# Halves of a head as even and odd channels: the regrouping of v's weights as 32-bit words on VectorE

## The chip, the core and the metric

One core of one Trainium2 chip runs the kernel. The metric is the device time of one execution in microseconds (us), as the median of three runs.

## The reference, cut to what matters

Two independent parts share one output of 2048 rows: columns 0 to 575 are part A, a sliding attention of 32 heads with 18 channels each, over 8 positions at a distance of 2; columns 576 to 1151 are part B, a long convolution.

```python
S, D, H, Dh, W, dil = 2048, 576, 32, 18, 8, 2
q, k, v = heads(x @ wqkv)                      # part A
logits = einsum("bhsd,bhswd->bhsw", q, k[idx]) * Dh ** -0.5      # idx = s - 2w, masked below 0
o = einsum("bhsw,bhswd->bhsd", softmax(logits), v[idx])
a = o.reshape(B, S, D) @ wo
k_shift = sum of 4 shifted copies of k, each times shift_k       # part B
kv = k_shift * v
b = q * (causal_convolution(kv, ssm_k) + kv * ssm_D)             # by FFT in the reference
```

## The kernel before, in words

TensorE (PE) multiplies, VectorE (DVE) makes elementwise products, ScalarE (ACT) evicts PSUM and does exponentials, GpSimd (POOL) and SyncE (SP) issue DMAs.

Part A. x is transposed to xT. `project` (L377 to L411) makes q, k and v transposed, 128 channels by 1024 positions at a time, in PSUM tiles ps_proj that ACT evicts (L411). For the logits, DVE multiplies q by shifted k (L827, 20 products, 10 for each half of the positions), PE sums the products over the 18 channels of a head into ps_log (L842), and ACT evicts ps_log (L847). `softmax` (L870 to L887) works on DVE, with the exponential (L876), the logarithm (L883) and its negative exponential (L884) on ACT. DMAs of SP spread the weights (L931). DVE multiplies them by v (L953), PE sums over the 8 positions into ps_acc (L970, L984), and ps_wo (L1025, L1017) multiplies by wo, which six DMAs of POOL load (L1001, L1004).

For that product a head's 18 channels of v are held as two halves, 9 channels each: partition 2h + s holds half s of head h, one channel of the half in each group of 64. So the columns of v's weights must stand in another order than in memory. They land raw in the tile Ks, and `regroup` (L895) copies them into xw: five instructions of ACT, one for each block of 128 rows, each 128x576 bf16 read with a stride of 9 elements (18 bytes). Half 0 is channels 0 to 8 of a head, half 1 channels 9 to 17, and the rows of wo are loaded in the same order.

Part B. DVE applies the four taps (L574, L578, L594); PE folds (ps_fold, evicted at L606); the filter is folded as well (ps_rev, evicted at L673); matrices of sines turn both into spectra: `filter_spectrum` (ps_fk, L624 and L625, evicted at L690) and `x_spectrum` (ps_fx, L771, evicted at L773). Each spectrum has two parts and their sum as a third. The sum is made by DMAs, or by DVE at once in a whole add of 128x2304 (`add_third`, L1058), or, where that has not been done when the first product of a block needs it, in a piece of 128x768 (L1240). DVE multiplies spectra (L1095), PE sums products into ps_z (L1122) and transforms back (ps_inv L1154, ps_back L1195), and DVE multiplies by q.

The order of each engine's work is that in which the code issues it. Units of PE work with their evictions wait in a queue, `units`. The code calls `until()` at some 47 places, and the table PLACES says how many units are issued at each. FKS and FXS say how x spectra, filter spectra and projections of v stand behind each other in the queue, AT where the folds stand, PRE and ZMIX where the whole adds and the first products of spectra stand between the last products with v. REGROUP says where the five regroups stand in the queue. PSUM tiles come in two kinds, A and B, of two tiles each; ps_proj and ps_rev use A, ps_log and ps_acc B, and the spectra either.

Of the kernel before, what the change touches and what calls it, by code (L numbers as in the profile page):

```python
# [18 lines left out]
ZMIX = (  # L19
    1, 1, 2, 0, 0, 6,  # L20
)

PRE = (
    22, 16,
)

THIRDS = ((0, 1),), ((0, 2), (1, 2)), ((0, 3), (1, 3))

REGROUP = (
    2, 0, 0, 17, 17,  # L30
)

PLACES = (
    4, 19, 7, 8, 3, 0, 6, 4, 8, 3, 12, 3, 3, 1, 4, 4, 3, 4, 2, 4, 0, 5, 5, 6, 2, 4, 3, 2, 1, 0, 3, 1, 2, 2, 3, 1,
    0, 3, 2, 8, 10, 3, 0, 1, 13, 1, 1, 0,
)

FKS = (
    6, 0, 0, 0, 0, 0, 0, 0, 0, 0, 0, 0, 0, 0, 0, 0, 0, 0, 0, 0, 1, 0, 0, 2, 0, 0, 0, 0, 0, 0,
)  # L40
FXS = (
    7, 0, 0, 5, 1, 0, 0, 6, 1,
)

EARLY = (
# [1 line left out]
)  # L47

AT = (
    0, 5, 31,  # L50
)
# [8 lines left out]
def kernel(  # L60
# [13 lines left out]
    nc = tc.nc  # L74
    Bsz, S, D = A_x.shape
# [50 lines left out]
    xw = main.tile([128, 12 * HB], BF16, name="xw")  # L126
# [11 lines left out]
    def xT(kb, t0, n):  # L138
        return view(xw, HB * (3 + 3 * (t0 // 1024)) + 1024 * kb + t0 % 1024, [[1, n]])
# [41 lines left out]
    Ks = main.tile([128, 12 * HB], BF16, name="Ks")  # L181
# [3 lines left out]
    def k_at(m, part):  # L185
        return 3 * HB * (3 - m) + HB * part
# [128 lines left out]
    q, k = qk[:, 0:4 * S + 1024], qk[:, 4 * S + 1024:]  # L315
# [56 lines left out]
    def project(comp, jj):  # L372
        def body(ps, ct, jj, jp, first):
            for kb in range(4):
                se = dict(start=(kb == 0 and not first), stop=(kb == 3 and first))
                if ct < 4:
                    nc.tensor.matmul(ps[:, jp, :], wq(kb, comp, 128 * ct, 128), xT(kb, 1024 * jj + 512 * jp, 512), **se)  # L377
                    continue
                for e in range(2):
                    w = wq(kb, comp, 512, 64)  # L380
                    nc.tensor.matmul(ps[64 * e:64 * e + 64, jp, :], w, xT(kb, 1024 * (jj if ct < 4 else e) + 512 * jp, 512),
                                     tile_position=(0, 64 * e), **se)

        def tails(ps, ct, jj, first):
            se = dict(start=first, stop=not first)
            if ct < 4:
                for r in range(2):
                    nc.tensor.matmul(ps[:, r, :], wq(4, comp, 128 * ct, 128)[64 * r:64 * r + 64],  # L388
                                     x5(jj)[64 * r:64 * r + 64], tile_position=(64 * r, 0), **se)
                return  # L390
            for e in range(2):
                w = wq(4, comp, 512, 64)
                for r in range(2):
                    nc.tensor.matmul(ps[64 * e:64 * e + 64, r, :], w[64 * r:64 * r + 64],
                                     x5(jj if ct < 4 else e)[64 * r:64 * r + 64], tile_position=(64 * r, 64 * e), **se)

        def unit(ct, jj, jp, first, box):
            t, o, pad = dest(comp, ct)
            if jp == 0:
                box["ps"] = bank2("ps_proj", "A")  # L400
                if first:
                    tails(box["ps"], ct, jj, True)
            ps = box["ps"]
            body(ps, ct, jj, jp, first)
            if jp == 0:
                clk["P"] += 1.15 if first else 0.9
                return
            if not first:
                tails(ps, ct, jj, False)
            pe(0.9 if first else 1.15, "A", 1.02)  # L410
            nc.scalar.activation(view(t, o + pad + 1024 * jj, [[512, 2], [1, 512]]), ps[:], ACT.Copy)  # L411
            if ct == 4 and comp > 0:
                (nc.gpsimd if comp == 1 else nc.sync).dma_start(view(t, o, [[1, PAD]])[64:128, :], view(t, o + 1024, [[1, PAD]])[0:64, :])

        for ct in range(4) if jj < 2 else [4]:
            first = ct % 2 == 1 if ct < 4 else comp == 1
            box = {}
            for jp in range(2):
                units.append((0.9 + 0.25 * (jp != first), partial(unit, ct, jj % 2, jp, first, box),
                              f"v{jj}{ct}" if comp == 2 else f"proj{comp}"))  # L420
# [208 lines left out]
    def row(m, c):  # L629
        return kTok(m)[0:1, c, :]  # L630
# [20 lines left out]
    def negate(*ms):  # L651
        for m in ms:
            signed.add(m)
            dve(288, lambda: nc.vector.tensor_scalar(minus_of(m), spare(m) if m < 2 else row(m, 0), -0.5 * ROOT, None,
                                                     ALU.mult))
# [26 lines left out]
    def filter_spectrum(m):  # L682
        def unit(gi, cs):
            tag = filler_tag("fk", "AAB") if logits_run[0] else "A"
            ps = bank2("ps_fk", tag)
# [4 lines left out]
            nc.scalar.activation(view(Ks, k_at(m, cs ^ (m & 1)) + 96 * gi, [[768, 3], [384, 2], [1, 96]]), acc3(ps),  # L690
                                 ACT.Copy, scale=(PSG, MSG)[cs][m] * 2.0 ** 1.5 / 1024.0)
# [23 lines left out]
    raw = view(Ks, k_at(0, 0), [[D, 5], [1, D]])  # L715

    for i in range(NBL):
# [30 lines left out]
        for n, u in enumerate(mirrors):  # L748
            n = AT[n] if n < 2 else AT[i]
# [140 lines left out]
    def steps(gen, n):  # L890
        for _ in range(n):
            next(gen, None)

    def regroup(kb):
        nc.scalar.activation(view(xw, w_at(kb, 2), [[64, 9], [1, 64]]), view(raw, D * kb, [[1, 9], [9, 64]]), ACT.Copy)  # L895
        clk["A"] += 0.65

    until()
    la, lb = logits(0), logits(1)
    logits_run[0] = True  # L900
    for kb in range(5):
        units.insert(REGROUP[kb], (0.0, partial(regroup, kb), "regroup"))
    steps(la, 3)
    negate(1, 0)
    steps(la, 10)
    steps(lb, 1)
    sa = softmax(0, view(av, 2048, [[1, 1024]]), view(av, 3072, [[1, 512]]))
    steps(sa, 1)
    steps(lb, 3)
    steps(sa, 1)  # L910
    steps(lb, 1)
    steps(sa, 1)
# [84 lines left out]
    wo = view(qk, WO, [[2 * D, 2], [D, 2], [1, D]])  # L997
    woh = view(qk, WO + 4 * D, [[1, D]])
    for e in range(2):
        for b in range(2):  # L1000
            nc.gpsimd.dma_start(wo[64 * e:64 * e + 64, :, b, :],  # L1001
                                bass.AP(tensor=A_wo.tensor, offset=A_wo.offset + ((0, 3), (2, 1))[e][b] * D,
                                        ap=[[9 * D, 64], [4 * D, 2], [1, D]]))
# [338 lines left out]
```

## Time and profile before

| what | us |
|---|---|
| median of 3 runs (range) | 215.75 (215.73 to 215.81) |
| the profiled execution | 215.78 |
| its span, first to last instruction | 214.0 |
| PE busy | 200.8 |
| DVE busy | 191.0 |
| ACT busy | 156.4 |
| POOL busy | 72.0 |

The busy times are sums over one profiled execution. A matmul's end is modelled, so a busy PE need not be at its peak. Times within the execution count from the span's start. In rows of single instructions the square bracket at the end is the idle time of the engine just before the instruction, with what ended it.

### The profile page before, as it was taken

Reading aid. Unit: us, or ns where it says so; the run is one execution under the profiler, and the core shown is the slowest. Engines: PE = TensorE matmul, PEld = TensorE weight load, DVE = VectorE, ACT = ScalarE, POOL = GpSimd, SP = SyncE. Lnnn points to the kernel's source line nnn. Section 1 sums busy time; section 2 is a strip of 40 time slices with the busy share of each in tenths; the row PEclk is TensorE's granted clock in tenths of the full one; section 3 lists DMA queues with packets and bytes.
Section 4 is the critical chain, followed back from the end, with each engine's and each line's share of the span. In section 5 each row is a group of like instructions: output and inputs, shape, how many; then the busy total and the mean of one; then the engine's idle time right before and its main releaser. Section 6 shows DMA issues by size and latency. Waiting matters only on the chain.

```text
span 214.0 us, 5106 instructions
## 1 busy us (share of the span) xinstructions
PE 200.8 (94%) x2122; PEld 111.6 (52%) x2122; DVE 191.0 (89%) x142; ACT 156.4 (73%) x223; POOL 72.0 (34%) x107
## 2 busy tenths in 40 slices
PE   7999999999877898999999999999989999999891
PEld 3543443445644555563336456655655667676560
DVE  7989999999979987766989999899999869979981
ACT  3799975686899999975459868855765887575640
POOL 8999992102292509220074000002009204033000
PEclk9999999999999999999999999999999999999997
DMA  6999999899566416999979989395659996965233
GB/s 209 292 321 228 279 321 296 204 162 191 124 83 87 63 23 93 192 161 187 231 172 237 197 181 219 69 205 180 140 196 298 246 307 143 214 188 161 87 110 110
DMA packets 35332, 39.66 MB, mean 185 GB/s; under 512 B 17555, under 2 KB 28943, under 8 KB 35310
## 3 DMA queue, kind: packets, MB, share of 16 engines
q1 hardware_dynamic: 26812, 24.88, 47.0%
q0 software_dynamic: 6032, 11.95, 29.6%
q10 hardware_dynamic: 2466, 2.51, 3.7%
q8 instruction: 16, 0.26, 0.5%
q14 instruction: 6, 0.05, 0.1%
HBM read 13.11 MB, written 4.72 MB: 83 GB/s over the span
## 4 chain that ended last, share of the span: by engine, by line
PE 55%; ACT 10%; DVE 1%; issue 1%; DVEq 0%
PE ps_z L1122 9%; PE ps_wo L1025 8%; PE ps_inv L1154 7%; PE ps_acc L970 7%; PE ps_proj L377 7%; PE ps_fx L771 5%; ACT Ks L690 4%; PE ps_log L842 3%; PE ps_fk L624 2%; PE ps_wo L1017 1%; ACT qk L974 1%; PE ps_proj L388 1%; ACT xw L895 1%; PE ps_acc L984 1%; DVE TB L1163 1%; ACT av L847 1%
## 5 line engine op out<-in xcount | busy, mean ns | idle before, releaser
L377 PE MATMUL ps_proj<-xw 128*128 128x512 bf16 x160 | 37.6, 380 | 0.5 <-ACT TI L456 0.5
L827 DVE TENSOR_TENSOR av<-qk 128x4096 bf16<-128x4096 bf16 (+1 forms) x16 | 31.9, 2020 | 4.9 <-PE ps_log L842 4.7
L377 PEld LDWEIGHTS <-xw 128*128 128x128 bf16 x160 | 14.5, 97 | 19.7 <-issue 4.6
L690 ACT ACTIVATE Ks<-ps_fk 128x576 bf16<-128x576 f32 x32 | 19.4, 737 | 1.3 <-PE ps_fk L625 1.0
L411 ACT ACTIVATE qk<-ps_proj 128x1024 bf16<-128x1024 f32 x14 | 14.4, 1026 | 7.9 <-PE ps_proj L388 3.6
L1095 DVE TENSOR_TENSOR qk<-xw,Ks 128x2304 bf16<-128x2304 bf16 x14 | 18.5, 1354 | 1.3 <-PE ps_z L1122 1.2
L574 DVE TENSOR_TENSOR tB<-kj,skb 128x4608 bf16<-128x4608 bf16 (+1 forms) x8 | 19.3, 2418 | 0.1
L1135 ACT ACTIVATE av<-ps_z 128x768 bf16<-128x768 f32 x20 | 15.3, 809 | 5.4 <-PE ps_z L1122 5.4
L773 ACT ACTIVATE xw<-ps_fx 128x576 bf16<-128x576 f32 x32 | 19.1, 667 | 0.2 <-PE ps_fx L771 0.2
L771 PE MATMUL ps_fx<-xw,TB 128*128 128x288 bf16 x128 | 17.9, 287 | 1.3 <-ACT xw L606 1.2
L624 PE MATMUL ps_fk<-Ks,TB 128*128 128x384 bf16 x62 | 16.7, 326 | 1.9 <-ACT Ks L673 0.9
L1051 POOL DMA_DIRECT2D Ks<-Ks x3 | 3.6, 1217 | 43.4 <-PE ps_wo L1025 32.3
L1025 PE MATMUL ps_wo<-qk 128*128 128x288 bf16 x128 | 17.9, 287 | 0.0
L411 ACT ACTIVATE v<-ps_proj 128x1024 bf16<-128x1024 f32 x9 | 9.5, 1055 | 8.8 <-PE ps_proj L377 5.4
L771 PEld LDWEIGHTS <-TB 128*128 128x128 bf16 x128 | 11.8, 98 | 7.6 <-issue 4.5
L970 PE MATMUL ps_acc<-av,ident 64*64 64x512 bf16 x160 | 15.3, 378 | 0.0
L625 PE MATMUL ps_fk<-Ks,TB 128*128 128x192 bf16 x62 | 15.2, 245 | 0.0
L1025 PEld LDWEIGHTS <-qk 128*128 128x128 bf16 x128 | 11.5, 98 | 5.7 <-issue 3.0
L1157 ACT ACTIVATE v<-ps_inv 128x576 bf16<-128x576 f32 (+1 forms) x14 | 9.5, 675 | 6.6 <-PE ps_inv L1154 6.6
L1154 PE MATMUL ps_inv<-av,TI 128*128 128x288 bf16 (+1 forms) x96 | 13.6, 293 | 0.6 <-ACT av L1135 0.6
L953 DVE TENSOR_TENSOR av<-Ks,v 128x4096 bf16<-128x4096 bf16 x6 | 13.6, 2287 | 0.6 <-PE ps_acc L970 0.6
L974 ACT ACTIVATE qk<-ps_acc 128x1024 bf16<-128x1024 f32 x8 | 8.2, 1023 | 7.5 <-PE ps_acc L970 7.5
(199 smaller groups left out, 473.9 us busy)
## 6 DMA issues: line engine op xcount, KB each, us to landing
Ks<-Ks POOLq DMA_DIRECT2D x9, 576.0 KB, 7.0
TB<-av SPq DMA_DIRECT2D x12, 256.0 KB, 5.4
kj<-in_B_k_dram SPq DMA_DIRECT2D x6, 504.0 KB, 6.2
vt<-in_B_v_dram SPq DMA_DIRECT2D x8, 288.0 KB, 5.1
Ks<-av SPq DMA_DIRECT2D x8, 256.0 KB, 5.6
Ks<-Ks SPq DMA_DIRECT2D x3, 576.0 KB, 5.1
Ks<-in_A_x_dram SPq DMA_DIRECT2D x2, 576.0 KB, 5.2
xw<-in_A_wqkv_dram SPq DMA_DIRECT2D x2, 576.0 KB, 5.9
```

Source lines behind the costliest of these rows:

```text
L377: nc.tensor.matmul(ps[:, jp, :], wq(kb, comp, 128 * ct, 128), xT(kb, 1024 * jj + 512 * jp, 512), **se)
L411: nc.scalar.activation(view(t, o + pad + 1024 * jj, [[512, 2], [1, 512]]), ps[:], ACT.Copy)
L574: dve(2304 * n, lambda: nc.vector.tensor_tensor(to, view(kj, row * D, [[D, n], [D, 4], [1, D]]), view(skb, row * D, [[D, n], [0, 4], [1, D ...
L624: nc.tensor.matmul(o[:, 0:2], w, rhs[:, 0:2], start=start, stop=stop)
L690: nc.scalar.activation(view(Ks, k_at(m, cs ^ (m & 1)) + 96 * gi, [[768, 3], [384, 2], [1, 96]]), acc3(ps), ACT.Copy, scale=(PSG, MSG)[cs][ ...
L771: nc.tensor.matmul(ps[:, pm, 0:HD], TX[:, 2 * pm + c, 128 * gi:128 * gi + 128], kv[:, 2 * c + pm, HD * h:HD * h + HD], start=(c == 0), sto ...
L773: nc.scalar.activation(view(xw, HB * XG[i] + 96 * gi + 1152 * h, [[HB, 2], [384, 3], [1, 96]]), view(ps, 0, [[512, 2], [96, 3], [1, 96]]), ...
L827: return P, at, step, dve(1024 * nj, lambda: nc.vector.tensor_tensor(view(P, at, [[step, 4], [256, nj], [1, 256]]), view(t, o + 256 * hh, ...
L970: nc.tensor.matmul(acc[64 * o:64 * o + 64, h, :], ident[64 * h:64 * h + 64, 64 * h:64 * h + 64], view(P, 256 * u, [[2048, 2], [1, 256]])[6 ...
L1025: nc.tensor.matmul(ps[:, r, 0:HD], oT(hh, 2 * c + r, t)[:, o:o + 128], wo[:, t // 2, t % 2, HD * h:HD * h + HD], start=(t == 0 and h == 0) ...
L1122: nc.tensor.matmul(view(acc[r], 512 * h, [[192, 2], [96, 2], [1, 96]])[o:o + 64], w[64 * h:64 * h + 64, 64 * h:64 * h + 64], pr[64 * h:64 ...
L1154: nc.tensor.matmul(ps[:, c, 0:n], TI[:, sl, pm, 128 * c:128 * c + 128], Y(j, pm)[:, sl, c0:c0 + n], start=(pm == 0 and sl == 0), stop=(sl ...
```

## The change

The halves of a head become its even and its odd channels. Two neighbouring channels of 16 bits then are one word of 32 bits, and both halves keep the order of the words: the regroup copies words (0..8, head) in place of single channels. It is done by DVE with a bitwise or with zero, four blocks of 128 rows in one instruction (128x1152 words) and the fifth in another (128x288), each read with a stride of 9 words (36 bytes). ACT's five instructions go. The two are called just ahead of the first unit that projects v, or ahead of a unit of the last filter's spectrum, or at a place in the list of steps, whichever comes first. wo is loaded in the matching order of rows, in ten DMAs in place of six. Eight tables have other numbers.

```diff
 REGROUP = (
-    2, 0, 0, 17, 17,
+    15, 14,
 )
...
 FXS = (
-    7, 0, 0, 5, 1, 0, 0, 6, 1,
+    0, 0, 15, 0, 8, 0, 0, 4, 0,
 )
...
             if jp == 0:
                 box["ps"] = bank2("ps_proj", "A")
+                while comp == 2 and regroups:
+                    regroups.pop(0)()
...
-    def regroup(kb):
-        nc.scalar.activation(view(xw, w_at(kb, 2), [[64, 9], [1, 64]]), view(raw, D * kb, [[1, 9], [9, 64]]), ACT.Copy)
-        clk["A"] += 0.65
-
+    def regroup(k0, n):
+        src, to = (view(t, at, [[1, n * D]]).bitcast(I32) for t, at in ((Ks, k_at(0, 0) + D * k0), (xw, w_at(k0, 2))))
+        dve(576 * n, lambda: nc.vector.tensor_single_scalar(
+            to.rearrange("p (k a h) -> p k a h", k=n, a=9), src.rearrange("p (k h a) -> p k a h", k=n, a=9), 0,
+            ALU.bitwise_or))
+
+    regroups.extend([partial(regroup, 0, 4), partial(regroup, 4, 1)])
...
-            nc.gpsimd.dma_start(wo[64 * e:64 * e + 64, :, b, :],
-                                bass.AP(tensor=A_wo.tensor, offset=A_wo.offset + ((0, 3), (2, 1))[e][b] * D,
-                                        ap=[[9 * D, 64], [4 * D, 2], [1, D]]))
+            for u in range(2):
+                nc.gpsimd.dma_start(wo[64 * e:64 * e + 64, u, b, :],
+                                    bass.AP(tensor=A_wo.tensor, offset=A_wo.offset + (((0, 6), (4, 2))[e][b] + 8 * u) * D,
+                                            ap=[[18 * D, 32], [D, 2], [1, D]]))
```

What the tables move is seen in the order of the engines' instructions (line, operation, out<-in, size, and how often in a row). ACT before, from the first regroups, behind the last fold and three evictions of ps_fx, to the row ahead of the second eviction of logits; one L690 and that L847 follow:

```order
L773 ACTIVATE xw<-ps_fx 128x2x3x96 x3
L895 ACTIVATE xw<-Ks 128x576 x2
L773 ACTIVATE xw<-ps_fx 128x2x3x96 x2
L895 ACTIVATE xw<-Ks 128x576
L773 ACTIVATE xw<-ps_fx 128x2x3x96
L690 ACTIVATE Ks<-ps_fk 128x6x96 x2
L673 ACTIVATE Ks<-ps_rev 128x576 x2
L690 ACTIVATE Ks<-ps_fk 128x6x96
L847 ACTIVATE av<-ps_log 128x1024
L690 ACTIVATE Ks<-ps_fk 128x6x96 x7
L895 ACTIVATE xw<-Ks 128x576 x2
L673 ACTIVATE Ks<-ps_rev 128x576 x2
```

ACT now, from the same fold to the second eviction of logits (L414 is L411 of before, L778 is L773, L695 is L690, L676 is L673, L852 is L847):

```order
L414 ACTIVATE v<-ps_proj 128x1024 x2
L778 ACTIVATE xw<-ps_fx 128x2x3x96
L695 ACTIVATE Ks<-ps_fk 128x6x96
L778 ACTIVATE xw<-ps_fx 128x2x3x96
L695 ACTIVATE Ks<-ps_fk 128x6x96
L676 ACTIVATE Ks<-ps_rev 128x576 x2
L852 ACTIVATE av<-ps_log 128x1024
L695 ACTIVATE Ks<-ps_fk 128x6x96 x8
L676 ACTIVATE Ks<-ps_rev 128x576 x2
L695 ACTIVATE Ks<-ps_fk 128x6x96
L852 ACTIVATE av<-ps_log 128x1024
```

The regroups are gone, four of six evictions of ps_fx have moved behind, and two projections of v have come forward, to the place behind the last fold.

DVE now, where the taps of part B end (the L597) and the logits begin; before, the two L901 are not there and the other rows are the same:

```order
L597 TENSOR_TENSOR xw<-xw,vt 128x2304
L657 TENSOR_SCALAR Ks<-Ks 1x576 x2
L901 TENSOR_SCALAR xw<-Ks 128x1152
L901 TENSOR_SCALAR xw<-Ks 128x288
L832 TENSOR_TENSOR av<-qk 128x4096 x2
L832 TENSOR_TENSOR v<-qk 128x4x1024
L657 TENSOR_SCALAR Ks<-Ks 1x576
```

Both regroups stand ahead of the first logits product.

DVE before, where the first products of spectra (L1095) come between the last products with v (L953):

```order
L1058 TENSOR_TENSOR xw<-xw 128x2304
L953 TENSOR_TENSOR av<-Ks,v 128x4096 x2
L953 TENSOR_TENSOR qk<-TB,v 128x4096
L1240 TENSOR_TENSOR Ks<-Ks 128x768
L1095 TENSOR_TENSOR Ks<-xw,Ks 128x2304
L953 TENSOR_TENSOR av<-TB,v 128x4096
L1058 TENSOR_TENSOR Ks<-Ks 128x2304
L1095 TENSOR_TENSOR Ks<-xw,Ks 128x2304
```

DVE now at the same place (L1062 is L1058 of before, L956 is L953, L1244 is L1240, L1099 is L1095):

```order
L956 TENSOR_TENSOR av<-Ks,v 128x4096 x2
L956 TENSOR_TENSOR qk<-TB,v 128x4096
L1244 TENSOR_TENSOR Ks<-Ks 128x768
L1244 TENSOR_TENSOR xw<-xw 128x768
L1099 TENSOR_TENSOR Ks<-xw,Ks 128x2304
L956 TENSOR_TENSOR av<-TB,v 128x4096
L1062 TENSOR_TENSOR xw<-xw 128x2304
L1244 TENSOR_TENSOR Ks<-Ks 128x768
L1099 TENSOR_TENSOR Ks<-xw,Ks 128x2304
L956 TENSOR_TENSOR av<-TB,v 128x4096
L956 TENSOR_TENSOR qk<-TB,v 128x4096
L1062 TENSOR_TENSOR Ks<-Ks 128x2304
```

The whole adds of xw and Ks have moved behind, and there are three pieces of 128x768 in place of one.

More of the change, by code (lines that the diff above doesn't have):

```diff
@@ L19 @@
 ZMIX = (
-    1, 1, 2, 0, 0, 6,
+    2, 1, 1, 0, 1, 4,
 )
 PRE = (
-    22, 16,
+    25, 22,
 )
@@ L29 @@
 REGROUP = (
-    2, 0, 0, 17, 17,
+    15, 14,
 )
 PLACES = (
-    4, 19, 7, 8, 3, 0, 6, 4, 8, 3, 12, 3, 3, 1, 4, 4, 3, 4, 2, 4, 0, 5, 5, 6, 2, 4, 3, 2, 1, 0, 3, 1, 2, 2, 3, 1,
-    0, 3, 2, 8, 10, 3, 0, 1, 13, 1, 1, 0,
+    2, 14, 13, 4, 3, 0, 2, 4, 8, 2, 10, 2, 6, 1, 4, 4, 3, 6, 1, 3, 0, 5, 5, 5, 3, 3, 4, 2, 1, 0, 3, 11, 2, 2, 3,
+    1, 1, 4, 0, 10, 0, 3, 0, 2, 11, 1, 1, 0,
 )
 FKS = (
-    6, 0, 0, 0, 0, 0, 0, 0, 0, 0, 0, 0, 0, 0, 0, 0, 0, 0, 0, 0, 1, 0, 0, 2, 0, 0, 0, 0, 0, 0,
+    5, 1, 0, 0, 0, 0, 0, 0, 0, 0, 0, 0, 0, 0, 0, 3, 0, 0, 0, 0, 0, 0, 0, 0, 0, 0, 0, 0, 0, 0,
 )
 FXS = (
-    7, 0, 0, 5, 1, 0, 0, 6, 1,
+    0, 0, 15, 0, 8, 0, 0, 4, 0,
 )
@@ L49 @@
 AT = (
-    0, 5, 31,
+    1, 5, 19,
 )
@@ L109 @@
     pp = ctx.enter_context(tc.tile_pool(name="pp", bufs=2, space=PSUM))
+    regroups = []
     turns = {"fk": 0, "fx": 0, "wo": 0}
@@ L684, in unit @@
             tag = filler_tag("fk", "AAB") if logits_run[0] else "A"
+            while m == 0 and regroups:
+                regroups.pop(0)()
             ps = bank2("ps_fk", tag)
@@ L900 @@
     logits_run[0] = True
[L901 to L906, printed above, removed]
-    sa = softmax(0, view(av, 2048, [[1, 1024]]), view(av, 3072, [[1, 512]]))
[L908 to L912, printed above, removed]
+    sa = softmax(0, view(av, 2048, [[1, 1024]]), view(av, 3072, [[1, 512]]))
+    order = [la] * 3 + [partial(negate, 1, 0)] + [la] * 7 + [lb, sa, lb, lb, lb, sa, lb, sa]
+    for n, step in enumerate(order):
+        for at in REGROUP:
+            if n == at and regroups:
+                regroups.pop(0)()
+        step() if callable(step) else next(step, None)
     need("fk0")
@@ L1000 @@
         for b in range(2):
-            nc.gpsimd.dma_start(wo[64 * e:64 * e + 64, :, b, :],
-                                bass.AP(tensor=A_wo.tensor, offset=A_wo.offset + ((0, 3), (2, 1))[e][b] * D,
-                                        ap=[[9 * D, 64], [4 * D, 2], [1, D]]))
+            for u in range(2):
+                nc.gpsimd.dma_start(wo[64 * e:64 * e + 64, u, b, :],
+                                    bass.AP(tensor=A_wo.tensor, offset=A_wo.offset + (((0, 6), (4, 2))[e][b] + 8 * u) * D,
+                                            ap=[[18 * D, 32], [D, 2], [1, D]]))
         nc.gpsimd.dma_start(woh[64 * e:64 * e + 64, :],
-                            bass.AP(tensor=A_wo.tensor, offset=A_wo.offset + 8 * D, ap=[[9 * D, 64], [1, D]]))
+                            bass.AP(tensor=A_wo.tensor, offset=A_wo.offset + 16 * D, ap=[[18 * D, 32], [D, 2], [1, D]]))
     nst = [0]
```

## The prediction

> **What bounds the kernel now.** I read the profile's page first, then busy time by stage, then the chain of work that ended last, and last the rows of single engines in order of time.
>
> ```profile
> span 214.0 us, 5106 instructions
> PE 200.8 (94%) x2122; PEld 111.6 (52%) x2122; DVE 191.0 (89%) x142; ACT 156.4 (73%) x223; POOL 72.0 (34%) x107
> ```
>
> TensorE (PE) is busy for 200.8 of 214.0 us. It can only be made to wait less. By stage (columns: stage, its length, then busy time of PE, PEld, DVE, ACT and POOL, granted clock, DMA share, GB/s):
>
> ```profile
> 54.50:60.00 5.50, 4.55 (x41) 2.91 (x40) 5.50 (x6) 4.82 (x10) 2.58 (x5) 1.00 0.29 83
> 60.00:81.60 21.60, 18.24 (x176) 10.47 (x176) 17.87 (x12) 21.11 (x32) 9.88 (x13) 1.00 0.46 63
> 81.60:96.00 14.40, 13.75 (x126) 8.38 (x126) 10.99 (x10) 13.17 (x22) 6.57 (x7) 1.00 0.97 161
> 96.00:110.00 14.00, 14.00 (x106) 5.47 (x104) 11.11 (x6) 7.48 (x10) 1.42 (x3) 1.00 0.92 192
> 110.00:135.00 25.00, 24.93 (x262) 14.26 (x258) 24.86 (x15) 20.59 (x31) 4.55 (x6) 1.00 0.93 201
> 135.00:168.00 33.00, 32.26 (x440) 19.29 (x432) 32.15 (x20) 21.84 (x32) 7.56 (x9) 1.00 0.73 195
> 168.00:190.00 22.00, 21.98 (x353) 14.69 (x346) 18.14 (x15) 16.11 (x26) 4.02 (x5) 1.00 0.89 206
> ```
>
> From 54.5 to 96 PE idles 0.95 + 3.36 + 0.65 = 4.96 us. From 96 to 190 it idles 0.83 in all. From 60 to 81.6 ScalarE (ACT) is busy 21.11 of 21.60 us: ACT bounds that stage. The chain of waits says the same (start, length, what):
>
> ```profile
> 73.26 2.52 ACT Ks L690 x5
> ...
> 76.62 0.95 ACT xw L895
> 77.58 0.05 issue
> 77.62 1.38 ACT xw L895
> ...
> 80.63 0.93 ACT av L847
> ...
> 81.58 0.22 DVE av L870
> ```
>
> Evictions of PSUM, two regroups of v's weights (L895), then the logits' eviction (L847), and only then can VectorE (DVE) begin the softmax at 81.58. The change touches just this queue.
>
> **The change, part by part.** *Regroups leave ACT, other work is placed there.* Groups of ACT by line and shape (count, busy us, mean ns):
>
> ```profile
> L690 ACT ACTIVATE Ks<-ps_fk 128x576 bf16<-128x576 f32 x32 | 19.4, 737 | 1.3 <-PE ps_fk L625 1.0
> L773 ACT ACTIVATE xw<-ps_fx 128x576 bf16<-128x576 f32 x32 | 19.1, 667 | 0.2 <-PE ps_fx L771 0.2
> L411 ACT ACTIVATE v<-ps_proj 128x1024 bf16<-128x1024 f32 x9 | 9.5, 1055 | 8.8 <-PE ps_proj L377 5.4 <-PE ps_proj L388 3.4
> L895 ACT ACTIVATE xw<-Ks 128x576 bf16<-128x576 bf16 x5 | 6.3, 1319 | 0.0
> ```
>
> The five regroups are 6.3 us of the full queue. By the rows of the two orders, ACT's list between the last folds and the second eviction of logits has before 6 of L773, 5 of L895, 11 of L690, 4 of L673 and 2 of L847; afterwards it has 2 of L773, 2 evictions of v, and the same 11, 4 and 2. ACT saves 6.3 + 4 x 0.667 - 2 x 1.055 = 6.9 us, so it needs some 14 of the 21.6 us and bounds this stage no more.
>
> What PE does there instead, and where it waits now (start, length, instruction, idle before and releaser):
>
> ```profile
> 55.77 0.41 PE L670 MATMUL ps_rev<-Ks,flip 128*128 128x288 bf16 x2 [0.68 <-ACT Ks L673]
> 60.92 1.63 PE L771 MATMUL ps_fx<-xw,TB 128*128 128x288 bf16 x12 [1.19 <-ACT xw L606]
> 68.52 0.40 PE L670 MATMUL ps_rev<-Ks,flip2r 128*128 128x288 bf16 x2 [1.05 <-ACT xw L773]
> 70.25 0.32 PE L624 MATMUL ps_fk<-Ks,TB 128*128 128x384 bf16 x1 [0.54 <-ACT Ks L673]
> 75.62 1.05 PE L842 MATMUL ps_log<-av,E 128*32 128x512 bf16 x16
> 86.49 1.92 PE L381 MATMUL ps_proj<-xw 128*64 128x512 bf16 x16
> 88.34 0.41 PE L394 MATMUL ps_proj<-xw 64*64 64x512 bf16 x4
> 96.32 1.89 PE L377 MATMUL ps_proj<-xw 128*128 128x512 bf16 x8
> 108.99 0.39 PE L388 MATMUL ps_proj<-xw 64*128 64x512 bf16 x2
> ```
>
> Two projections of v come forward into the stage: 1.92 + 0.41 for the last 64 channels and 1.89 + 0.39 for a full group, together 4.6 us less some 0.2 of overlap between rows. Four units of the x spectrum (16 matmuls, at 1.63 / 12 each: 2.2 us) go out. So PE does 2.2 us more before the same point. A projection's eviction asks ACT for 1.055 us per 2.2 us of PE; a unit of the spectrum asks 0.667 per 0.54. The first projection also stands where PE waited 1.19 us: it needs no folded input.
>
> *The regroups on DVE.* Two instructions, 1152 and 288 words of 32 bits, now stand ahead of the first logits product. No row shows a 32-bit copy with a stride of 36 bytes. DVE's rows in that stage, and the two nearest groups with POOL's:
>
> ```profile
> 54.87 4.48 DVE L827 TENSOR_TENSOR av<-qk 128x4096 bf16<-128x4096 bf16 x2
> 62.41 0.30 DVE L654 TENSOR_SCALAR xw<-Ks 1x576 bf16<-1x576 bf16 x1 [0.61 <-DMA Ks<-Ks]
> 63.20 3.43 DVE L827 TENSOR_TENSOR av<-qk 128x4096 bf16<-128x4096 bf16 x2 [0.49 <-PE ps_log L842]
> 71.50 2.29 DVE L827 TENSOR_TENSOR av<-qk 128x4096 bf16<-128x4096 bf16 x1 [0.46 <-PE ps_log L842]
> 76.08 3.43 DVE L827 TENSOR_TENSOR av<-qk 128x2048 bf16<-128x2048 bf16 x2
> 81.58 0.21 DVE L870 TENSOR_TENSOR av<-av,maskb 32x128 bf16<-32x128 bf16 x1 [2.08 <-ACT av L847]
> ```
>
> ```profile
> L436 DVE TENSOR_SCALAR Ks<-Ks 128x1024 int32<-128x1024 int32 x4 | 2.8, 710 | 0.1
> L1240 DVE TENSOR_TENSOR Ks<-Ks 128x768 bf16<-128x768 bf16 x1 | 0.6, 554 | 0.0
> ```
>
> From below: L436 moves 1024 contiguous words in 0.710 us, in proportion 1440 words in 1.0. From above: L895 reads the same data at a stride of 18 bytes at 1319 / 576 = 2.29 ns an element; 1440 words at that are 3.3 us. I take the engine and word size of L436 and the worth of the stride from ACT, L895 against L690 of the same size, 1319 / 737 = 1.8: 1.0 x 1.8 = 1.8 us.
>
> [...]
>
> What is queued behind these 1.8 us is every logits product, and PE's ps_log and the softmax wait for those. But DVE's own waits before 79.5 are 0.61 + 0.49 + 0.46 = 1.56 us: the first is for a row copied by DMA that would by then have landed, the others for PE's reads of a buffer, which were held up by ACT's queue. I let all three go. The tenth product (the 128x2048 at 76.08) then ends 1.8 - 1.56 = 0.24 later than now, at about 77.6; PE's 1.05 and ACT's 0.93 for the logits follow behind one rev and one fk eviction, and the softmax starts near 80.5, 1.1 us ahead of 81.58. So at the second logits PE stands at the time where it stands now (0.2 us either way) with 2.2 us more done: the gain, 2.2. Over the regroup's bounds it is 3.0 (1.0 us) to 0.7 (3.3 us).
>
> *From there to 110.* ACT stays nearly full from 81.6 to 96 (13.17 of 14.40): behind the softmax's start the list keeps 16 filter evictions up to the second exponential row, loses one projection (1.055) and gains two spectrum units (1.33). I expect PE's 0.65 us of waits there to stay. DVE must keep step: it idles 3.41 + 2.89 = 6.3 us from 81.6 to 110, waiting for PE and ACT, so a PE that is 2.2 us ahead takes it along.
>
> *After 110*, both PE and DVE are full. Before, the sum for the first block of xw was taken ahead of the first product and only that of Ks needed a piece of its own (L1240); afterwards both sums come behind the first product, and two pieces more of 128x768 are made: 2 x 0.554 = 1.1 us of DVE. DVE's slack is 0.14 + 0.85 us up to 168 and 3.86 from 168 to 190, so I put between 0 and 1.1 on the path, and take 0.3. The large add for xw (L1058) moves behind DVE's products for two ps_acc, which speaks for the small value.
>
> *The rest.* The reordered folds before 54.5 keep PE's work; each follows its taps. The last projections now come between the last fold and the first rev, so that ACT has one short eviction less in front of rev's: of the 0.68 us before 55.77 I count 0.5 as gone (0 to 0.68). The load of wo is ten DMAs on POOL instead of six, for rows that the first ps_wo reads at 139.69; POOL stands before its next DMA of another kind for 32.3 us:
>
> ```profile
> 139.69 1.14 PE L1025 MATMUL ps_wo<-qk 128*128 128x288 bf16 x8
> ...
> 108.58 1.26 POOL L1001 DMA_DIRECT2D qk<-in_A_wo_dram  x2 [13.62 <-DVE av L827]
> 146.87 1.19 POOL L1051 DMA_DIRECT2D Ks<-Ks  x1 [32.32 <-PE ps_wo L1025]
> ```
>
> Four more at 0.63 are 2.5 us, some 20 us ahead of that read: nothing, and 2.5 us if that cover were gone. Order of the output rows costs nothing: the same matmuls.
>
> Sum: -2.2 - 0.5 + 0.3 = -2.4 us. The profiled execution took 215.78 us (span 214.0 and 1.78 around it), 0.03 above the median of the runs shown, so I keep its scale: 215.8 - 2.4 = 213.4.
>
> **The rivals.** *DVE takes over (slower).* DVE's time before the stage is full (5.50 of 5.50 from 54.5), and after 110 it is full. If its waits up to 110 keep their size, because PE's ps_log still come when other units let them, then the regroup lies wholly on the path with the extra pieces: 1.8 + 1.1 = 2.9, up to 3.3 + 1.1 = 4.4. It decides once fewer than 2.9 of the 1.56 + 2.08 + 6.3 = 9.9 us of waits go. Against it: 2.08 of them are plainly ACT's. Time: 217 to 220, 218.0 in the middle.
>
> *The gain is given back (no change to small gain).* The projections that filled the wait are missing later: from 81.6 to 96, PE has a projection less to put between filter units, each of which costs ACT 0.6 and PE 0.5 us, so that PE waits for ACT there by what it won. For it: ACT's 13.17 of 14.40. Against it: two spectrum units and ACT's own 1.2 us of slack. Time: 214.6 to 216.2, 215.3 in the middle.
>
> *All waits go.* ACT freed of 6.9 us lets PE fill all 4.96 us: 210.8. Against it: DVE's products pace PE's ps_log from 57 to 78.
>
> That the regroup does not happen where the list says is excluded: the first unit that projects v calls both, so that the places 15 and 14 of the table find nothing left.
>
> **How the numbers follow.** My forecast (a gain of 1.2 to 3.8: 212.0 to 214.6) has 0.54, all waits gone (to 210.8) 0.08, the gain given back 0.21, slower 0.17. About 0.2% (0.43 us) is what a measurement of this kernel can tell from no change. Of the given-back case about half lies below 215.35 and half in 215.35 to 216.2. Faster: 0.54 + 0.08 + 0.11 = 0.73; same 0.10; slower 0.17. The range leaves out some 0.04 of the fastest and 0.14 of the slowest: 211.3 to 216.8.
>
> **What would show it.** Right: no wait of PE at the place of 60.92, DVE's two regroups at 54.9 with 1.8 us together, the softmax's first row (now 81.58) near 80.5, ACT under 90% busy from 60 to 80, and the first ps_acc about 2.5 us earlier than now for equal work. Wrong: regroups of 3 us and PE waiting for DVE before each ps_log (DVE as bound), or PE idle by over 2 us between 80 and 97 (given back). If the start of the softmax does not move, the first step is wrong; if it does and the end does not, look after 110.

## The result, and the profile after

| kernel | median us | lowest to highest | runs |
|---|---|---|---|
| before, on the same chip | 215.74 | 215.72 to 215.81 | 4 |
| after | 212.56 | 212.09 to 213.95 | 4 |
| after, unaltered, a second time (the run called control) | 212.09 | 212.07 to 212.44 | 4 |

The ratio is 0.9863 (95% interval 0.9817 to 0.9909) in the first set and 0.983 (0.9817 to 0.9842) in the second, where before had 23 runs. The kernel is faster by 3.2 to 3.65 us; 2.4 was forecast. The four executions of the first set lie 1.9 us apart, those of the second 0.4, and no trace shows what the one of 213.95 met. The profiled execution of after took 212.5 us, 3.28 less than the 215.78 of before; that of the control took 212.08.

The page of after, first its span and the busy time of each engine:

```profile
span 210.8 us, 5106 instructions
PE 200.1 (95%) x2114; PEld 110.7 (53%) x2122; DVE 193.1 (92%) x146; ACT 150.5 (71%) x218; POOL 74.0 (35%) x111
```

PE's work is the same: both record 2122 weight loads (PEld), and after has eight matmuls fewer only because some records are missing. DVE has 2.1 us more to do and ACT 5.9 less, and the span is 3.2 shorter. By stage, with the columns of before's table:

```profile
54.50:60.00 5.50, 5.12 (x46) 3.36 (x47) 5.50 (x7) 4.34 (x8) 2.03 (x4) 1.00 0.40 106
60.00:81.60 21.60, 21.46 (x202) 11.72 (x200) 21.46 (x17) 17.14 (x29) 12.20 (x14) 1.00 0.56 76
81.60:96.00 14.40, 13.52 (x119) 8.35 (x118) 11.28 (x7) 13.46 (x24) 4.80 (x4) 1.00 0.94 159
96.00:110.00 14.00, 13.80 (x103) 5.59 (x104) 11.90 (x8) 7.39 (x8) 4.81 (x9) 1.00 0.96 210
110.00:135.00 25.00, 24.81 (x293) 14.94 (x295) 24.72 (x14) 20.59 (x33) 2.97 (x3) 1.00 0.87 186
135.00:168.00 33.00, 32.17 (x434) 19.90 (x429) 32.68 (x23) 22.23 (x33) 7.57 (x9) 1.00 0.80 210
```

From 54.5 to 96 PE now idles 0.38 + 0.14 + 0.88 = 1.40 us where it idled 4.96: 3.56 less. Nearly all of that lies in the one stage that ACT had bounded. From 96 to 168 the same sum gives 0.20 + 0.19 + 0.83 = 1.22 where it gave 0.81, but part of this is no wait: a matmul whose record is missing leaves a gap too (0.16 at 96.04, in a row of 3 instead of 4). Rows of equal work are safer. These stand behind 1827 weight loads each, in before and in after:

```profile
189.90 3.12 PE L1154 MATMUL ps_inv<-av,TI 128*128 128x288 bf16 x24
```

```profile
186.12 3.11 PE L1158 MATMUL ps_inv<-av,TI 128*128 128x288 bf16 x24
```

PE is 3.78 us ahead there. From 60 to 81.6 ACT was busy 21.11 us of the 21.60, and is now busy 17.14; PE (21.46) and DVE (21.46) are both full instead.

PE's rows in the order of time: every wait between 54 and 97, the projection that took the place of the wait at 60.92, and the second logits.

```profile
54.53 0.41 PE L673 MATMUL ps_rev<-Ks,flip 128*128 128x288 bf16 x2 [0.28 <-ACT qk L414]
55.67 0.41 PE L673 MATMUL ps_rev<-Ks,flip 128*128 128x288 bf16 x2 [0.25 <-ACT Ks L676]
59.73 1.92 PE L382 MATMUL ps_proj<-xw 128*64 128x512 bf16 x16
77.60 0.60 PE L847 MATMUL ps_log<-av,E 128*32 128x512 bf16 x8
87.10 0.32 PE L627 MATMUL ps_fk<-Ks,TB 128*128 128x384 bf16 x1 [0.70 <-ACT Ks L695]
96.04 0.81 PE L378 MATMUL ps_proj<-xw 128*128 128x512 bf16 x3 [0.16 <-issue]
```

Between 56 and 87 PE waits for nobody. (The row at 96.04 is the one with the missing record.) DVE in the same stretch, the regroups first:

```profile
55.02 1.75 DVE L901 TENSOR_SCALAR xw<-Ks 128x1152 int32<-128x1152 int32 x2
56.70 4.47 DVE L832 TENSOR_TENSOR av<-qk 128x4096 bf16<-128x4096 bf16 x2
...
63.87 3.40 DVE L832 TENSOR_TENSOR av<-qk 128x4096 bf16<-128x4096 bf16 x2
...
76.00 3.41 DVE L832 TENSOR_TENSOR av<-qk 128x2048 bf16<-128x2048 bf16 x2
79.34 0.21 DVE L875 TENSOR_TENSOR av<-av,maskb 32x128 bf16<-32x128 bf16 x1
```

None of these rows has a bracket any more. The tenth product of this half (at 76.00; before at 76.08) comes at the old time although 1.7 us of regroups stand ahead of it, and the softmax follows at 79.34 instead of 81.58.

### The profile page after: what moved, and what is told of

Read it like the earlier page. It is cut to its first block, busy times and chain, and to the rows that moved or that the text cites. A ratio compares the mean times of both kernels' runs of the same rounds, so it can differ in the third digit from the quotient of the medians.

```text
span 210.8 us, 5106 instructions
## 1 busy us (share of the span) xinstructions
PE 200.1 (95%) x2114; PEld 110.7 (53%) x2122; DVE 193.1 (92%) x146; ACT 150.5 (71%) x218; POOL 74.0 (35%) x111
## 4 chain that ended last, share of the span: by engine, by line
PE 80%; ACT 10%; DVE 5%; issue 2%; DVEq 0%; ACTq 0%
PE ps_proj L378 16%; PE ps_z L1126 9%; PE ps_wo L1029 8%; PE ps_acc L973 7%; PE ps_inv L1158 7%; PE ps_fx L776 6%; PE ps_log L847 4%; PE ps_proj L500 3%; PE ps_fk L627 3%; PE ps_proj L382 3%; PE ps_proj L389 3%; ACT Ks L695 3%; PE ps_rev L673 2%; PE ps_fk L628 1%; ACT qk L977 1%
## 5 line engine op out<-in xcount | busy, mean ns | idle before, releaser
L378 PEld LDWEIGHTS <-xw 128*128 128x128 bf16 x160 | 14.0, 97 | 20.5 <-issue 6.2
L1099 DVE TENSOR_TENSOR qk<-xw,Ks 128x2304 bf16<-128x2304 bf16 x14 | 18.5, 1355 | 2.5 <-PE ps_inv L1158 2.4
L414 ACT ACTIVATE qk<-ps_proj 128x1024 bf16<-128x1024 f32 x14 | 14.3, 1023 | 7.6 <-PE ps_proj L389 3.3
L695 ACT ACTIVATE Ks<-ps_fk 128x576 bf16<-128x576 f32 x32 | 18.6, 717 | 1.3 <-PE ps_fk L628 1.3
L778 ACT ACTIVATE xw<-ps_fx 128x576 bf16<-128x576 f32 x32 | 18.4, 666 | 0.0
L414 ACT ACTIVATE v<-ps_proj 128x1024 bf16<-128x1024 f32 x9 | 9.3, 1029 | 9.3 <-PE ps_proj L378 4.3
L977 ACT ACTIVATE qk<-ps_acc 128x1024 bf16<-128x1024 f32 x8 | 8.2, 1024 | 8.0 <-PE ps_acc L973 8.0
L956 DVE TENSOR_TENSOR av<-Ks,v 128x4096 bf16<-128x4096 bf16 x6 | 13.6, 2286 | 0.2 <-PE ps_acc L973 0.2
```

Source lines behind the costliest of these rows:

```text
L1099: r = dve(3 * QTR, lambda: nc.vector.tensor_tensor(pr, view(xw, HB * XG[i] + QTR * t, [[HB, 3], [1, QTR]]), view(Ks, k_at(j - i, 0) + QTR ...
```

## The experiments

Times are medians, and each ratio is against runs of before in the same set: before took 215.74 us beside the control and the first three kernels, 216.03 beside *no_regroup*, *regroup_twice*, *sums_early* and *spectra_first*, and 216.00 beside the last three. "Control" is after unaltered, 212.09 us. The main theory is that the gain comes from ACT's queue: the regroups leave it, and PE's projections fill PE's wait.

**Which half of the change does what.** Two kernels each make one part alone. *new_order_act_late* keeps the new order and layout, but ACT does the regroup, in five instructions that copy pairs of channels, at the place where the two of DVE stood in the list; they then come ahead of the first eviction of v.

```diff
-        dve(576 * n, lambda: nc.vector.tensor_single_scalar(
+        def copies():
+            for kb in range(k0, k0 + n):
+                nc.scalar.activation(view(xw, w_at(kb, 2), [[64, 9], [2, 32], [1, 2]]),
+                                     view(raw, D * kb, [[2, 9], [18, 32], [1, 2]]), ACT.Copy)
+        dve(576 * n, copies)
```

> The changed order and layout, but the regroup is five ACT instructions again, all ahead of the first eviction of v. Theory (ACT's queue was the limit): five times 1.25 us stand in ACT's list where PE has to wait for them before the first projection of v, so PE idles some 5 us after 60 and the time is 217 to 219. Rival (the new order alone brings the gain, whichever engine regroups): 212.3 to 213.5.

Measured: 216.84 us (215.89 to 217.79 in 12 runs), ratio 1.0037 (1.0019 to 1.0055): slower than before, as the queue theory said, though just under its 217 to 219. The rival, that the order alone brings the gain, falls. PE's rows, from the profiled execution of 217.13 us:

```profile
62.02 0.41 PE L382 MATMUL ps_proj<-xw 128*64 128x512 bf16 x2 [2.33 <-ACT xw L902]
62.61 0.41 PE L382 MATMUL ps_proj<-xw 128*64 128x512 bf16 x2 [0.19 <-ACT xw L902]
63.22 0.41 PE L382 MATMUL ps_proj<-xw 128*64 128x512 bf16 x2 [0.19 <-ACT xw L902]
63.82 2.07 PE L382 MATMUL ps_proj<-xw 128*64 128x512 bf16 x10 [0.20 <-ACT xw L902]
```

The order that gains 3.6 us with DVE loses 1.1 against before when its first projection has to wait for ACT. The size came out near in part by luck: the expectation had five copies of 1.25 us and some 5 us of waits, but in pairs of channels they took 738 ns each, and the waits are 2.91 us. What else the loss consists of is told under the hardware, below.

*old_order_dve* is the other half: the order of before, with the two word copies on DVE ahead of the first logits product, the word layout and its ten loads of wo.

```diff
+    regroup(0, 4)
+    regroup(4, 1)
...
-        units.insert(REGROUP[kb], (0.0, partial(regroup, kb), "regroup"))
+        units.insert(REGROUP[kb], (0.0, partial(nothing, kb), "regroup"))
```

> The order of before, but the regroup is the two DVE instructions ahead of the first logits product, with the word layout and ten loads of wo; ACT's five are gone. Theory (ACT's queue was the limit): ACT falls from 21.1 to about 15 us in 60 to 81.6, PE loses the waits of 1.05, 0.54 and 0.37 us but keeps that of 1.19 at 60.9, and the time is 213.3 to 214.5. Rival (the order alone): DVE's 1.75 us are added and nothing is won, 215.7 to 217.5.

Measured: 213.76 us (213.48 to 216.44 in 12 runs), ratio 0.9933 (0.9908 to 0.9958). So the move off ACT alone is worth 1.98 us by the medians, and 0.9 to 2.0 by the interval, since four of the twelve took 214.94 or more; the new order adds 1.67 by the medians. The stage says where the rest is left, and PE's rows say why:

```profile
60.00:81.60 21.60, 19.46 (x188) 11.41 (x188) 21.38 (x17) 17.77 (x31) 10.75 (x14) 1.00 0.56 76
```

```profile
60.90 1.63 PE L771 MATMUL ps_fx<-xw,TB 128*128 128x288 bf16 x12 [1.19 <-ACT xw L606]
66.14 0.61 PE L842 MATMUL ps_log<-av,E 128*32 128x512 bf16 x8 [0.51 <-DVE av L827]
69.36 0.32 PE L624 MATMUL ps_fk<-Ks,TB 128*128 128x384 bf16 x1 [0.54 <-ACT Ks L673]
```

The wait of 1.19 us for the folded x is still there at 60.9: ACT's lighter list doesn't remove it, only work that needs no folded input does. Of the other three that were expected to go, the 1.05 and the 0.37 are gone and the 0.54 is not. PE idles 2.14 us in the stage, between 3.36 (before) and 0.14 (after).

**Is it the engine, or the place on it?** *new_order_act_early* takes the same five ACT copies, but spreads them over the gaps that ACT has from 46 to 56 us, behind the 11th to 14th evictions of q and k.

```diff
+            evicted[0] += 1
+            for _ in range({11: 1, 12: 2, 13: 1, 14: 1}.get(evicted[0], 0)):
+                kb = early_blocks.pop(0)
+                nc.scalar.activation(view(xw, w_at(kb, 2), [[64, 9], [2, 32], [1, 2]]),
...
```

> The changed order and layout, but the regroup is five ACT instructions spread over the last evictions of q and k, between 44 and 55, where ACT idles over 0.5 us after each eviction. Theory (what counts is that the regroup leaves ACT's full stage from 60 to 82, not which engine does it): 212.0 to 213.0, the same as the changed kernel, with DVE 1.75 us less busy. Rival (DVE is the better engine for words, the gain hangs on it): 214 or more. A second rival (DVE's 1.75 us are on the path of the changed kernel): 210.8 to 211.5.

Measured: 212.75 us, ratio 0.9861 (0.9848 to 0.9874), 0.66 over the control and inside the 212.0 to 213.0 of the queue theory. DVE, without the regroup, has a wait in its place:

```profile
64.34 3.43 DVE L837 TENSOR_TENSOR av<-qk 128x4096 bf16<-128x4096 bf16 x2 [2.52 <-ACT v L414]
```

The 0.66 come from the eviction of the last q and k: it starts at 54.16 instead of the control's 53.44, because copies stand ahead of it, and the softmax follows as much later (80.04 instead of 79.31). So the engine matters little and the place much: the same five instructions cost 0.66 us at 46 to 56 and 4.75 at 61.2.

**Is DVE's regroup hidden?** *no_regroup* leaves the regroup out: the weights of v go straight to their tile as they lie in memory, so v's columns come in another order and the values are others.

```diff
-            load_w(nc.sync, 2, raw)
+            load_w(nc.sync, 2)
...
+        dve(576 * n, lambda: None)
```

> The changed kernel without the two DVE regroups: v's weights are loaded straight to their place, so the columns of v stand in the order of memory. Theory (PE is the limit from 60 to 82 now, busy 21.46 of 21.6 us, and DVE's 1.75 us are covered): 211.7 to 212.3, with new DVE waits of over 1 us before 80. Rival (the regroup lies on DVE's path to the softmax): 210.3 to 210.9.

Measured: 212.07 us, ratio 0.9822 (0.9809 to 0.9834), against 212.09 with the regroup: nothing. Its one profile is of an execution of 961.28 us, which no theory here bears on, so the same kernel ran once more for its stages:

> The kernel without its regroup once more, for its stages (the weights of v go to their tile as they lie in memory, so v's columns come in another order). Covered regroup: PE's idle time from 54.5 to 81.6 stays between 0.3 and 0.9 us, the first row of the softmax starts within 0.3 us of 79.3, and DVE waits for PE or ACT where it now does its two instructions; the end is within 211.7 to 212.5. Rival, DVE in the way: the softmax starts over 1 us earlier.

It took 212.08 us, and DVE's rows show what lies in the regroup's place:

```profile
63.61 3.43 DVE L832 TENSOR_TENSOR av<-qk 128x4096 bf16<-128x4096 bf16 x2 [1.63 <-ACT v L414]
...
79.32 0.21 DVE L875 TENSOR_TENSOR av<-av,maskb 32x128 bf16<-32x128 bf16 x1
```

DVE stops for 1.63 us until 63.6, where it would have come anyway (63.87 in after). The profile names ACT's eviction of v, which ended at 63.18; PE's first ps_log, at 62.89 in this run, reads the buffers that these products write, so it may well be that one. Either way PE's order sets this time. The regroup, 1.68 us from its start to that of the next product, fills the 1.63 and a little more: the tenth product starts at 75.77 here, at 75.86 in the control and at 76.00 in after, but the softmax starts at 79.3 in all three. *regroup_twice* issues each of the two copies twice:

```diff
+        for _ in range(2):
             dve(576 * n, lambda: nc.vector.tensor_single_scalar(
```

> The changed kernel with each DVE regroup issued twice: 1.75 us more of DVE ahead of the logits. Both theories agree that DVE has no slack left there (no wait of 0.2 us from 55 to 79): the first softmax row moves from 79.3 to 80.6 to 81.1, PE gets waits before ps_log, and the time is 213.1 to 213.9. If it stays at 212.1 to 212.4, DVE has cover that the profile does not show.

Measured: 213.95 us, ratio 0.9903 (0.989 to 0.9916), 1.86 over the control for 1.97 us more of DVE. Time and softmax (81.28) are just later than the 213.9 and 81.1 expected. PE now waits for DVE:

```profile
68.12 0.61 PE L847 MATMUL ps_log<-av,E 128*32 128x512 bf16 x8 [1.20 <-DVE av L832]
```

So the first 1.75 us are free and the second 1.97 are paid but for 0.1. The rival "DVE takes over" was real, and begins just beyond the regroup's length.

**What the words are worth.** *regroup_bf16* keeps before's halves and its six loads of wo, and lets DVE copy single channels, by a plain copy in place of the bitwise or:

```diff
-        dve(576 * n, lambda: nc.vector.tensor_single_scalar(
+        dve(576 * n, lambda: nc.vector.tensor_copy(
```

> The regroup of before's layout (halves 0 to 8 and 9 to 17 of 18 as before, six loads of wo) on DVE, element by element in bf16: 2880 elements of 2 bytes in place of 1440 words. If an element costs what a word costs (0.8 to 1.3 ns), the two take 3.3 to 3.8 us in place of 1.75, and as the run with the regroup twice showed that what is over 1.75 is on the path, the end is 213.7 to 214.2. The rival: the price goes by bytes, 1.7 to 2.0 us, and the end is 211.9 to 212.6; then the 32-bit words bought nothing.

Measured: 213.46 us (213.42 to 213.71), ratio 0.988 (0.9849 to 0.9911): 1.37 over the control, under the 1.6 to 2.1 that the expected 213.7 to 214.2 stand for, which had taken the whole excess as paid; some 0.3 us of the 1.64 were still covered. Groups of DVE by line and shape, for this kernel and then for after:

```profile
L901 DVE COPY xw<-Ks 128x2304 bf16<-128x2304 bf16 x1 | 2.3, 2265 | 0.0
L901 DVE COPY xw<-Ks 128x576 bf16<-128x576 bf16 x1 | 1.2, 1197 | 0.0
```

```profile
L901 DVE TENSOR_SCALAR xw<-Ks 128x1152 int32<-128x1152 int32 x1 | 1.2, 1179 | 0.0
L901 DVE TENSOR_SCALAR xw<-Ks 128x288 int32<-128x288 int32 x1 | 0.6, 647 | 0.0
```

With the same bytes, twice the elements took 1.9 times as long (2265 / 1179, 1197 / 647), so the price went by elements and not by bytes, as far as copy and bitwise or are alike. The words save 1.64 us of DVE in a row and 1.37 at the end. *regroup_read_in_order* reads the words as they lie and writes them apart instead:

```diff
-            to.rearrange("p (k a h) -> p k a h", k=n, a=9), src.rearrange("p (k h a) -> p k a h", k=n, a=9), 0,
+            to.rearrange("p (k a h) -> p k h a", k=n, a=9), src.rearrange("p (k h a) -> p k h a", k=n, a=9), 0,
```

> The same words, but the instruction reads its words in the order of memory and writes them apart (steps of 32 words). Theory A (the price comes from reading apart): the two together cost nearer to the contiguous 0.69 ns a word plus a fixed part, 1.1 to 1.4 us in place of 1.75. Theory B (either side apart costs the same): 1.6 to 2.0 us. By both the end is within 211.9 to 212.6, since 1.75 us there cost nothing at the end. A dearer write, over 2.5 us, would show at the end as in the run with the regroup twice.

Measured: 212.08 us in one run, and:

```profile
L901 DVE TENSOR_SCALAR xw<-Ks 128x1152 int32<-128x1152 int32 x1 | 1.2, 1245 | 0.0
L901 DVE TENSOR_SCALAR xw<-Ks 128x288 int32<-128x288 int32 x1 | 0.4, 414 | 0.0
```

The two together take 1.50 us from start to end, between the theories: the large copy is no cheaper (theory B), the small one is (as theory A has it). In the large copy writing apart cost about as much as reading apart, 1245 ns against 1179; the small one is told of under the hardware.

**Do the later pieces cost?** *sums_early* sets the table PRE to 20, 16 in place of 25, 22. Then the whole adds stand earlier, no piece of 128x768 is made, and DVE has less to do after 110.

> The changed kernel with PRE at 20 and 16: both whole sums of the first block come before the first product, and the three pieces of 128x768 (1.66 us of DVE after 144) go. Theory (DVE's extra work after 110 lies beside PE's): 211.8 to 212.4. Rival (DVE is full from 110 to 168 and carries it to the end): 210.4 to 211.1.

Measured: 212.37 us (212.08 to 213.01), ratio 0.9835 (0.9819 to 0.9852). DVE is busy 30.99 us from 135 to 168 in place of 32.68, and the end does not move (212.08 in the profiled execution, as in the control's): the pieces cost nothing.

**Do the projections have to come first?** *spectra_first* is after with x spectra ahead of the projections again (FXS 7, 0, 1, 0, 8, 0, 0, 4, 0) and the regroup called directly ahead of the logits.

> The changed kernel with FXS at 7, 0, 1, 0, 8, 0, 0, 4, 0 and the regroup where it is: x spectra stand first in the queue again, the two projections of v that had come forward stand behind them. Theory (which units stand there is a gain of its own: projections need one eviction for 2.2 us of PE, and no folded input): PE's wait of over 1 us near 60.9 is back, and the time is 212.9 to 213.8. Rival (the regroup's leaving ACT and the other tables make the whole gain): 211.9 to 212.4.

Measured: 215.09 us, ratio 0.9963 (0.9949 to 0.9977): the rival falls, and the theory's 212.9 to 213.8 was too mild. The wait of the old order is back (1.19 at 60.94), with 1.03 at 66.20 for DVE, and PE idles 2.06 us from 60 to 81.6. The softmax still starts at 79.38, as in after, but PE has less done by then, and that shows later:

```profile
60.00:81.60 21.60, 19.54 (x192) 11.32 (x191) 21.46 (x17) 16.93 (x29) 11.53 (x14) 1.00 0.56 76
81.60:96.00 14.40, 13.46 (x119) 8.05 (x117) 10.01 (x7) 12.67 (x21) 4.80 (x4) 1.00 0.84 140
96.00:110.00 14.00, 13.32 (x99) 4.90 (x97) 10.27 (x6) 6.78 (x8) 2.28 (x5) 1.00 0.97 200
```

DVE does 20.28 us of work from 81.6 to 110 instead of 23.18: it waits for ps_log while the projections that should have been done catch up. By the stage windows PE idles 0.28 us more from 54.5 to 60, then 1.92, 0.06 and 0.49 in the three stages shown, and 0.16 and 0.12 in the two up to 168, against the control: together the 3.0. So the tables work only together: with x spectra first the new ones are 1.3 us behind *old_order_dve*, which has the old ones.

> The changed kernel once more, unaltered, to see how far its single runs lie apart (212.1 to 214.0 in four, against 215.72 to 215.81 of before). Every theory: median 212.3 to 212.9 and DVE's first softmax row near 79.3. If the spread is 1.5 us again, other kernels with this order are to be compared by their profiles' stages as well as by their medians.

The control came in at 212.09, just under the expected 212.3 to 212.9, with the waits of after in the same places up to 190. Behind that, after's profiled execution has a wait that neither the control nor before has, as DVE came 0.4 us later than in the control:

```profile
195.93 0.36 PE L1126 MATMUL ps_z<-qk,ident 64*64 64x384 bf16 x4 [0.32 <-DVE qk L1099]
```

That is most of the 0.42 us between the two profiled executions.

## Why the prediction was right, step by step, and where it was short

- *What bounds the stage*: right. ACT's queue from 60 to 81.6 was the bound, and the chain from its regroups to the softmax is gone. From 60 to 80 ACT is busy 15.54 of 20 us, under the 90% named as a sign. The estimate that ACT needs some 14 of the 21.6 us does not compare with the 17.14, since PE is 3 us further on by then and so brings ACT more.
- *The regroup on DVE at 1.8 us, covered by 1.56 us of waits*: right in size (1.75 measured), and the cover was larger. The tenth product starts 0.08 us earlier than before; the forecast had 0.24 later. By start times, DVE needs 21.21 us from 54.87 to 76.08 before, and 19.30 from 56.70 to 76.00 after. So 1.91 us of delay went and not 1.56: the brackets show only three of the stops, and not the small ones (0.09 us ahead of the tenth product) nor the overlap of instructions that DVE loses at each: by the rows' starts and lengths from 54.4 to 76.1, the next starts 0.06 to 0.09 us before the end of the one ahead where DVE doesn't stop. In the large copy a word took 1179 / 1152 = 1.02 ns, against 710 / 1024 = 0.69 in the contiguous copy of L436 in before. The upper end of 3.3 us was not reached.
- *"So at the second logits PE stands at the time where it stands now with 2.2 us more done"*: this is the step that was mis-sized. PE's row stands at 77.60 instead of 78.62 (before's row follows), with the same 2.2 us more done: 3.2. The forecast let the softmax follow 4.2 us behind the start of the tenth product (76.32 to 80.5), with PE and ACT taking their turn behind other units; it follows 3.34 us behind (76.00 to 79.34; before 5.50). Having shown that ACT was no longer the bound, it still charged a queue at ACT. In after the logits are done at 78.20, and their eviction stands behind one other alone, that ends at 78.27. The row of before, then ACT's two of after:

```profile
78.62 0.60 PE L842 MATMUL ps_log<-av,E 128*32 128x512 bf16 x8
```

```profile
77.61 0.66 ACT L695 ACTIVATE Ks<-ps_fk 128x576 bf16<-128x576 f32 x1
78.26 1.02 ACT L852 ACTIVATE av<-ps_log 128x1024 bf16<-128x1024 f32 x1
```

- *The wait ahead of rev, 0.5 of 0.68 gone*: too high, and counted on top. The wait became 0.28 + 0.25 = 0.53 in two places, so 0.15 was won. It lies ahead of the second logits, whose place the first term had already fixed, so that no term of its own belonged in the sum. That the forecast came as near as it did is in part luck: without this term it would have been -1.9.
- *Waits from 81.6 to 96 stay*: in that window nearly, 0.88 us instead of 0.65, mostly one wait of 0.70 for ACT. But the forecast's list of waits ended ahead of the second logits. Before has two more just behind, 1.18 us together, and after has the 0.70 in their place, so PE gains another 0.5:

```profile
79.60 0.32 PE L624 MATMUL ps_fk<-Ks,TB 128*128 128x384 bf16 x1 [0.37 <-ACT Ks L673]
82.14 0.32 PE L624 MATMUL ps_fk<-Ks,TB 128*128 128x384 bf16 x1 [0.81 <-ACT Ks L690]
```

  The rival in which the gain is given back there took at most 0.2 us.
- *0.3 us for DVE's pieces after 110*: none. The first product with v, a late filter product and the last product with ps_back, before and after, show it:

```profile
110.04 2.29 DVE L953 TENSOR_TENSOR av<-TB,v 128x4096 bf16<-128x4096 bf16 x1 [0.62 <-PE ps_log L842]
161.28 1.35 DVE L1095 TENSOR_TENSOR v<-xw,Ks 128x2304 bf16<-128x2304 bf16 x1
209.46 1.02 DVE L1163 TENSOR_TENSOR TB<-ps_back,TB 128x384 bf16<-128x384 f32 x2 [0.78 <-PE ps_back L1181]
```

```profile
106.68 2.29 DVE L956 TENSOR_TENSOR av<-TB,v 128x4096 bf16<-128x4096 bf16 x1 [0.62 <-PE ps_log L847]
158.73 1.35 DVE L1099 TENSOR_TENSOR v<-xw,Ks 128x2304 bf16<-128x2304 bf16 x1
206.19 1.02 DVE L1167 TENSOR_TENSOR TB<-ps_back,TB 128x384 bf16<-128x384 f32 x2 [0.78 <-PE ps_back L1185]
```

  DVE leads by 3.36 us, then by 2.55 (it has paid for the pieces), then by 3.27 again: its slack from 168 to 190 gives it back. *sums_early* agrees.
- *wo's ten loads*: no wait of PE at ps_wo shows in after. They were not tried apart from the rest.

The sum that the runs bear out is -3.2 at the second logits (rev's 0.15 is in it) and -0.5 just behind: -3.7, which fits the 3.78 that PE is ahead at 190 and the 3.65 to 3.70 of the control. After's own profiled execution lost 0.4 of it near 196 and shows 3.28. On record was -2.4. So the mechanism was right, and the term of the first logits stage was 1.0 us too small. Of the rivals, "all waits go" (210.8) came as near to the control as the forecast did, 1.3 us each; to the first set's 212.56 the forecast came nearer. From 60 to 81.6 the waits did nearly all go. "DVE takes over" was avoided by 0.1 to 0.3 us of cover, as *regroup_twice* and *regroup_bf16* show.

## What to carry to other kernels

The work that was moved to a fuller engine was free here as long as it lay in a wait that another engine's order set: 1.75 us of it cost nothing at the end, 1.97 more cost 1.86. Find that wait's length (leave the work out) and its edge (do it twice) before making the work longer or shorter. When a change takes an engine off the bound, take its queue out of every later step of the sum as well. And the copy's place counted for more than its engine or its price: the same five instructions cost 0.7 us in one place and 4.7 in another, part of which was the clock.

## What the runs showed of the hardware

**Behind a wait of PE the clock was halved.** In *new_order_act_late* PE stood from 59.7 to 62.0 and then ran with gaps. The granted clock is the number behind POOL's in its windows; up to 64 it is 1.00:

```profile
64.00:65.00 1.00, 1.00 (x8) 0.47 (x6) 0.00 (x0) 0.38 (x1) 1.00 (x4) 0.57 1.01 146
65.00:66.00 1.00, 1.00 (x10) 0.14 (x5) 0.00 (x0) 0.00 (x0) 0.54 (x3) 0.50 1.13 167
66.00:67.00 1.00, 1.00 (x5) 0.28 (x3) 0.00 (x0) 0.36 (x1) 0.00 (x0) 0.50 1.02 104
67.00:68.00 1.00, 0.78 (x6) 0.23 (x9) 0.00 (x0) 0.66 (x1) 0.00 (x0) 0.72 0.40 52
```

The lost clock is 0.43 + 0.50 + 0.50 + 0.28 = 1.7 us, and the waits are 2.33 + 0.19 + 0.19 + 0.20 = 2.9: together 4.6 of the 5.0 us by which this execution's span (215.4) is over the control's (210.4). So a third of the loss is no wait and stands in no bracket. Waits of 1.19 to 1.21 us in the other kernels (*old_order_dve*, *spectra_first*, *regroup_twice*, *regroup_bf16*) left the clock at 1.00, from 60 to 81.6 as a whole; in *new_order_act_late* that stage shows 0.92. Of the twelve executions five took 215.89 to 215.97 us with a mean clock of 0.994 to 0.995, and seven 216.64 to 217.79 with 0.987 to 0.992; it may be that only the seven met the halved clock, but a trace was taken of one alone. If the clock was at 0.50 or at 1.00 and nowhere between, the four windows stand for 0.86 + 1.00 + 1.00 + 0.56 = 3.4 us at 0.50, as an estimate. Ahead of them lie the wait of 2.33 us in one piece and three of 0.2. That these waits set it off is inferred from their place and was not varied.

**The strided word copy.** The two copies that read in order (1245 and 414 ns) fit a fixed part of 137 ns and 0.96 ns a word; this is worked out from just the two. With the same fixed part, the copies that read apart cost (1179 - 137) / 1152 = 0.90 ns a word with four blocks in one instruction, and (647 - 137) / 288 = 1.77 with one. In bf16 it is 0.92 and 1.84 an element. So the single block paid double when its outermost loop is the 9 words, and not when it is the 32 heads. Whether that is for the odd length of this loop or for something else in the order is open, as no run varied it alone.

**ACT's copy of pairs.** On ACT a regroup of 128x576 took 1304 ns (median) in before, element by element at 18 bytes, and 732 in *new_order_act_early*, where two neighbouring channels are read together: the layout by words alone, without a change of engine, nearly halves ACT's five copies. What before would gain from that alone, with ACT's list some 2.9 us shorter (5 x 0.57), was not tried.
